# RWKV-6 attention ahead of a token/channel mixer: the read-out by 128-token chunks in place of 256-token units

## The chip, the cores and the metric

The kernel runs on one core of one Trainium2 chip. The metric is the device time of one execution in microseconds (us). A time given for a part comes from one profiled execution, counted from the start of its span. The engines are named PE (TensorE matmul), PEld (TensorE weight load), DVE (VectorE), ACT (ScalarE), POOL (GpSimd) and SP (SyncE, which issues most transfers).

## The reference

The inputs r, k, v, w have shape (4 batches, 8 heads, 768 tokens, 48). Each head carries a 48×48 state through the tokens; the result, laid out as (4, 768, 384), goes through a mixer over tokens and one over channels.

```python
for t in range(S):
    cur = einsum('bhd,bhe->bhde', u[None] * k[t], v[t])
    y[t] = einsum('bhd,bhde->bhe', r[t], state + cur)
    state = w[t][..., None] * state + einsum('bhd,bhe->bhde', k[t], v[t])
# x = y as (batch, tokens, heads * 48)
h = maximum(x.T @ w_tok1, 0) @ w_tok2          # over tokens, 768 -> 256 -> 768
u = x + h.T
out = u + maximum(u @ w_ch1, 0) @ w_ch2        # over channels, 384 -> 1536 -> 384
```

The mixer's weights arrive as 64-bit floats and are converted to 32 bits on the chip.

## The kernel before

**The attention** is done in 12 units of 256 tokens, three for each batch (`NU`, `UB`). A unit has two chunks of 128 tokens (`UC`), a chunk has two blocks of 64 tokens (`T`). Heads are handled in four pairs (`A`): one head of a pair lies in partitions 0 to 47, the other in 64 to 111 (`P` is 64). In the code q is the head of the pair and j the block of the chunk.

`levels(i)` forms the weights of every token upon every other inside a block of 64. It doubles the block length step by step: `gram` multiplies k and r on TensorE (line 246, and line 232 for the first step), `join` multiplies decays into k, r and w on VectorE (lines 271 to 273), and `pick` moves the wanted part of the product into the tile `at` (VectorE lines 238 and 255, ScalarE line 263).

`post(i)` then makes the unit's output, in these pieces:

- `tokens` transposes k on TensorE (line 306) and copies it out with ScalarE (line 307) as `kT`.
- `carry` multiplies kT and v (line 316) into the PSUM tile `kv`: for each block of 64 tokens, what it adds to the state. `update` forms the states, one for every block, on VectorE (lines 330 and 333).
- `before` multiplies r with the states (line 353) into the PSUM tile `y`. ScalarE then reads one column of it into the small tile `seen` (line 359), which `within` waits for.
- `within` adds the weights inside a block times v (line 366) to `y`; ScalarE copies the sum to `x` (lines 370 and 372).

`kv` and `y` take turns in the pool `ps_a`, which has one buffer of two PSUM banks. All these matmuls use 64 rows and 64 columns of the 128×128 array at a time. [...] For `within` the function `put` decides the latter: block j of head q goes to output half `j ^ q`, and the copies of line 372 bring the halves of the second head back into place.

**The mixer** (`mixing(bt)`) of a batch is: `hidden` (h1, line 386), `back` (line 393, added to x on VectorE in line 395), `turn` (transposes, lines 400 and 401), `up` (z, lines 408 and 410) and `down` (h2, lines 417 and 421). These matmuls use the whole array.

**The weights** are converted by `convert`, two blocks of 128×512 at a time, in six steps on VectorE and ScalarE (lines 168 to 174), with four buffers for the raw words.

**The order.** Pieces carry a weight, and `woven` merges lists of pieces in proportion to these weights. For batch 0 the levels of units 0 and 1 come first; then the levels of unit 2 with `post` of units 0 and 1, and `post` of unit 2, each woven with conversion steps; the hidden matmuls of batch 0 are set in between as their x chunks come. The rest of batch 0's mixer follows, then with batch bt's mixer the attention of batch bt + 1 is woven in. The scheduler of the language may still move single instructions between pieces where their operands allow it, within each engine's queue[...]. Units are loaded three ahead (`load_rkw`, `load_v`, both on SP's queue, issued at the end of `post`).

## Time and profile before

| what | value |
|---|---|
| time, median of 3 runs | 661.45 us (660.84 to 664.48) |
| time of the profiled execution | 661.45 us |
| its span | 659.7 us |
| PE busy | 622.7 us (94%) |
| DVE busy | 273.5 us (41%) |
| ACT busy | 194.9 us (30%) |
| line 366, `within` on PE | 768 records of 384 matmuls |
| line 333, state on DVE | 160 operations, 29.1 us busy |

The span is the time from the first to the last instruction of the program that the profile shows; 1.75 us of the execution lie around it. A busy time is the union of an engine's instructions[...]. An f32 matmul leaves two records on PE and two on PEld. The "chain" follows the work back from the last instruction to what released it; its pieces add up to the span. The clock granted to TensorE is given as a share of full speed.

### The profile page before, as it was taken

To read this page: it belongs to the slowest core of one execution; us is meant where nothing else is said; L and a number is where in the kernel's file an instruction comes from. 1 tells how busy PE (TensorE), PEld (TensorE's weight loads), DVE (VectorE), ACT (ScalarE), POOL (GpSimd) and SP (SyncE) were. 2 spreads that over 40 slices of the span, in tenths; PEclk is the share of its full clock that TensorE was granted. 3 is DMA by queue.
4 is the path that set the end of the run, shared out by engine and by line. 5 is a ranking of instruction groups with operands and counts; after the bars stand their busy time and mean duration, and the time that the engine had idled before them with its cause. 6 is when DMAs were issued, how large, how long until landed. Compare 5 with 4: busy or idle time off the path is not lost.

```text
span 659.7 us, 18806 instructions
## 1 busy us (share of the span) xinstructions
PE 622.7 (94%) x8584; PEld 456.6 (69%) x8584; DVE 273.5 (41%) x618; ACT 194.9 (30%) x465; POOL 7.2 (1%) x32
## 2 busy tenths in 40 slices
PE   3889789999999899999999999999999999999997
PEld 3777557867866666787686666788687565886854
DVE  6889789935555326242252226243143111000000
ACT  7153554512350431423231313432121201230200
POOL 3000000000000000000000000000000000000000
PEclk9996779999999899999999999999999999999999
DMA  8236755501030320101202220000000000000000
GB/s 348 79 99 193 203 141 171 191 0 51 27 107 18 109 62 2 50 2 50 73 2 61 63 74 1 2 2 2 14 14 14 13 26 0 1 1 12 13 24 24
DMA packets 19375, 38.56 MB, mean 58 GB/s; under 512 B 2112, under 2 KB 12864, under 8 KB 19296
## 3 DMA queue, kind: packets, MB, share of 16 engines
q1 hardware_dynamic: 19152, 37.36, 18.0%
q8 instruction: 67, 1.10, 0.7%
q14 instruction: 12, 0.10, 0.0%
q10 hardware_dynamic: 144, 0.00, 0.0%
HBM read 32.64 MB, written 4.72 MB: 57 GB/s over the span
## 4 chain that ended last, share of the span: by engine, by line
PE 88%; DVE 5%; ACT 3%; DMA 2%; issue 1%; SPq 0%; DVEq 0%; ACTq 0%
PE z_ps L408 29%; PE h_ps L417 29%; PE gram L246 10%; PE h_ps L386 6%; PE h_ps L393 5%; PE y_ps L353 2%; PE y_ps L366 2%; PE gram L232 2%; PE kv_ps L316 2%; PE kT_ps L306 1%; ACT at L263 1%; DMA d<-in_w_ch_dram 1%; DVE r L272 1%; PE xT_ps L400 1%; DMA w<-in_rkw_dram 1%
## 5 line engine op out<-in xcount | busy, mean ns | idle before, releaser
L408 PE MATMUL z_ps<-xT,wch 128*128 128x256 f32 x864 | 197.2, 384 | 0.6 <-ACT xT L401 0.6
L417 PE MATMUL h_ps<-wch,z 128*128 128x384 f32 x576 | 192.9, 491 | 0.8 <-ACT kT L307 0.8
L408 PEld LDWEIGHTS z_ps<-xT,wch 128*128 128x128 f32 x864 | 160.8, 190 | 23.7 <-ACT xT L401 0.8
L417 PEld LDWEIGHTS h_ps<-wch,z 128*128 128x128 f32 x576 | 107.8, 190 | 72.0 <-ACT kT L307 1.2
L410 ACT ACTIVATE z<-z_ps 128x256 f32<-128x256 f32 x144 | 55.1, 383 | 172.2 <-PE z_ps L408 172.2
L421 DVE TENSOR_TENSOR o<-x,h_ps 128x384 f32<-128x384 f32 x24 | 13.3, 554 | 200.6 <-PE h_ps L417 200.6
L246 PEld LDWEIGHTS gram<-r,k 48*64 48x64 f32 x3840 | 74.7, 155 | 23.3 <-issue 16.1
L246 PE MATMUL gram<-r,k 48*64 48x32 f32 x3840 | 81.8, 237 | 7.7 <-issue 3.1
L271 DVE TENSOR_TENSOR k<-k,decay 112x512 f32<-112x512 f32 x36 | 24.9, 691 | 58.8 <-PE gram L246 58.8
L386 PE MATMUL h_ps<-x,wtok 128*128 128x384 f32 x96 | 40.4, 571 | 1.7 <-ACT x L372 1.6
L263 ACT COPY at<-gram 16x256 f32<-16x256 f32 (+1 forms) x72 | 31.3, 434 | 32.9 <-PE gram L246 31.5
L393 PE MATMUL h_ps<-h,wtok 128*128 128x384 f32 x96 | 36.5, 508 | 3.4 <-DVE x L395 1.7
L271 DVE TENSOR_TENSOR k<-k,w 112x512 f32<-112x512 f32 x36 | 24.7, 687 | 35.5 <-PE gram L246 30.2
L333 DVE SCALAR_TENSOR_TENSOR state<-state,w_chunk,kv_ps 128x48 f32<-128x48 f32 x160 | 29.1, 258 | 11.0 <-PE kv_ps L316 10.9
L255 DVE COPY_PREDICATED at<-mask,gram 128x512 f32<-128x512 uint8 x36 | 32.3, 897 | 0.0
L238 DVE COPY_PREDICATED at<-mask,gram 128x512 f32<-128x512 uint8 x24 | 16.3, 723 | 37.2 <-PE gram L232 37.1
L232 PE MATMUL gram<-rp,kp 48*64 48x64 f32 x768 | 21.3, 250 | 10.5 <-ACT kp L220 8.0
L232 PEld LDWEIGHTS gram<-rp,kp 48*64 48x64 f32 x768 | 17.5, 155 | 17.8 <-ACT kp L220 10.4
L386 PEld LDWEIGHTS h_ps<-x,wtok 128*128 128x128 f32 x96 | 19.9, 219 | 13.9 <-issue 3.3
L272 DVE TENSOR_TENSOR r<-r,w 112x512 f32<-112x512 f32 x36 | 24.5, 685 | 6.7 <-ACT rp L216 6.7
L393 PEld LDWEIGHTS h_ps<-h,wtok 128*128 128x128 f32 x96 | 16.6, 189 | 14.8 <-DVE x L395 2.9
L359 ACT COPY seen<-y_ps 128x2 f32<-128x2 f32 x12 | 1.9, 160 | 79.4 <-PE y_ps L353 79.4
(55 smaller groups left out, 388.0 us busy)
## 6 DMA issues: line engine op xcount, KB each, us to landing
d<-in_w_ch_dram SPq DMA_DIRECT2D x10, 512.0 KB, 4.6
vt<-in_v_dram SPq DMA_DIRECT2D x12, 384.0 KB, 3.7
out_dram<-o SPq DMA_DIRECT2D x24, 192.0 KB, 1.9
x<-in_w_ch_dram SPq DMA_DIRECT2D x8, 512.0 KB, 4.2
w<-in_rkw_dram SPq DMA_DIRECT2D x18, 192.0 KB, 3.4
k<-in_rkw_dram SPq DMA_DIRECT2D x18, 192.0 KB, 3.2
r<-in_rkw_dram SPq DMA_DIRECT2D x18, 192.0 KB, 3.4
d<-in_w_tok_dram SPq DMA_DIRECT2D x4, 512.0 KB, 9.5
```

Source lines behind the costliest of these rows:

```text
L232: pe.matmul(g[cols, q, ts(a, T)], L["kp"][rows, tokens], L["rp"][rows, tokens], start=True, stop=True)
L246: fours(lambda q, j, rows, cols: pe.matmul(g[cols, q, ts(ca, 32)], k_[rows, ds(ca * 128 + j * T, T)], right[rows, ts(2 * ca + j, 32 // b), ...
L255: dve.copy_predicated(out=dst, data=g.rearrange("p q (m b) -> p q m b", b=b), mask=masks[l].rearrange("p x t -> p (x t)").rearrange("p (m ...
L263: act.copy(at[p:p + b, :, :, n * 2 * b + b:(n + 1) * 2 * b], g[p:p + b, :, :, ts(n, b)])
L271: dve.tensor_mul(left, left, wv[:, :, 1].unsqueeze(2).to_broadcast([ROWS, n, b]))
L272: dve.tensor_mul(right, right, wv[:, :, 0].unsqueeze(2).to_broadcast([ROWS, n, b]))
L333: dve.scalar_tensor_tensor(new[:, a], state[bt, g][:, a], L["w"][:, c, a, j:j + 1], got[:, a], op0=ALU.mult, op1=ALU.add)
L386: pe.matmul(sums[i], wtok1[:, c, ts(i, 128)], xs[bt][:, c, :], start=(c == 0), stop=(c == C - 1))
L393: pe.matmul(ps, wtok2[:, i, ts(c, 128)], h1[:, i, :], start=(i == 0), stop=(i == DTOK // 128 - 1))
L408: pe.matmul(ps, wch1[:, m, ts(jt, 128)], xT[:, m, ts(s, SEG)], start=(m == 0), stop=(m == DM // 128 - 1))
L410: act.activation(zs[s][:, jt, :], ps, AF.Relu)
L417: pe.matmul(ps, zs[s][:, jt, ts(n, 128)], wch2[:, jt, :], start=(jt == 0), stop=(jt == NJ - 1))
```

## The change

`post` works chunk by chunk. The functions `tokens`, `carry`, `before` and `within` take the chunk c and do half of what they did; `update` is gone, its work is at the end of `carry`. In `before` and `within`, block j of both heads goes to output half j, and `put` is gone, so a single copy brings y of a chunk to x. The state takes a multiply with a broadcast decay and an add, each over all four head pairs, in place of four operations that did both for one pair. `seen` is copied by halves. There are six state buffers before and five after; `kT` holds one chunk and has two buffers. In batch 0 the last two pieces of unit 2 (`before` and `within` of its second chunk) are taken out of the woven list and stand ahead of the fifth pair of hidden pieces, and the loads of unit 5 come after that pair.

The change is listed under the words "Weight conversion with three two-input VectorE operations, exponent in 16 bits through ScalarE, two pieces side by side, four raw-word buffers". The diff does not touch `convert`, which is so in both kernels.

```diff
-        def tokens():
+        def tokens(c):
...
-            L["kT"] = apool.tile([128, UC, A, 128], f32, name="kT", bufs=1)
...
+            L["kT"] = apool.tile([128, A, 128], f32, name="kT")
+            act.copy(L["kT"], ps)
...
+        def carry(c):
             L, vt = live[i], vs[i]
-            kv = L["kv"] = ps_a.tile([128, 2, 512], f32, name="kv_ps", tag="a")
...
+            kv = ps_a.tile([128, 2, 512], f32, name="kv_ps", tag="a")
+            for a in range(A):
+                for j, q in ((0, 0), (1, 1), (0, 1), (1, 0)):
+                    if not (last and j == 1):
+                        pe.matmul(kv[ts(q, P), j, ts(a, D)], L["kT"][ts(j, T), a, ts(q, P)],
+                                  vt[ts(j, T), c, ts(2 * a + q, D)], start=True, stop=True)
+            for j in range(1 if last else 2):
+                g = 2 * ch + j
+                new = apool.tile([128, A, D], f32, name="state", bufs=5)
+                got = kv[:, j, :A * D].rearrange("p (a e) -> p a e", a=A)
+                if g == 0:
+                    dve.tensor_copy(new, got)
+                else:
+                    dve.tensor_mul(new, state[bt, g], L["w"][:, c, :, j].unsqueeze(2).to_broadcast([128, A, D]))
+                    dve.tensor_add(new, new, got)
+                state[bt, g + 1] = new
-        def update():
...
-                        for a in range(A):
-                            dve.scalar_tensor_tensor(new[:, a], state[bt, g][:, a], L["w"][:, c, a, j:j + 1], got[:, a],
-                                                     op0=ALU.mult, op1=ALU.add)
...
-        pairs = ((0, 0), (1, 0), (1, 1), (0, 1))
-
-        def put(q, j):
-            return ts(j ^ q, T)
+        pairs = ((0, 0), (1, 1), (1, 0), (0, 1))
...
+        def before(c):
...
+            for a in range(A):
+                for q, j in got:
+                    pe.matmul(y[ts(j, T), q, ts(a, D)], r_[q * P:q * P + D, ds((c * A + a) * 128 + j * T, T)],
+                              state[bt, 2 * ch + j][q * P:q * P + D, a, :], start=(a == 0), stop=False,
+                              skip_group_check=True)
             seen = apool.tile([128, 2], f32, name="seen")
-            act.copy(seen, y[:, :, UC * A * D - 1])
+            for j in range(2):
+                if (0, j) in got:
+                    act.copy(seen[ts(j, T)], y[ts(j, T), :, A * D - 1])
...
-                for q, j in ((0, 0), (0, 1), (1, 1), (1, 0)):
-                    pe.matmul(y[put(q, j), q, ts(ca, D)], at[ts(j, T), q, ca, :], vt[ts(j, T), c, ts(2 * a + q, D)],
-                              start=False, stop=ca == 0, skip_group_check=True)
...
-            act.copy(x[:, 0], got[:, 0])
-            for n in range(2):
-                act.copy(x[ts(n, P), 1], got[ts(1 - n, P), 1])
+            for a in reversed(range(A)):
+                for q, j in pairs:
+                    pe.matmul(y[ts(j, T), q, ts(a, D)], at[ts(j, T), q, c * A + a, :],
+                              vt[ts(j, T), c, ts(2 * a + q, D)], start=(2 * ch + j == 0 and a == A - 1), stop=a == 0,
+                              skip_group_check=True)
+            act.copy(xs[bt][:, ch, :].rearrange("p (a q e) -> p q a e", a=A, q=2),
+                     y[:, :, :A * D].rearrange("p q (a e) -> p q a e", a=A))
...
-        return [(1.0, tokens), (1.1, carry), (0.1, update), (1.1, before), (1.1, within),
-                (0.01, lambda: load_rkw(i + 3)), (0.01, lambda: load_v(i + 3))]
+        pieces = []
+        for c in range(UC):
+            pieces += [(0.5, lambda c=c: tokens(c)), (0.5, lambda c=c: carry(c))]
+        for c in range(UC):
+            pieces += [(0.5, lambda c=c: before(c)), (1.0, lambda c=c: within(c))]
+        return pieces + [(0.01, lambda: load_rkw(i + 3)), (0.01, lambda: load_v(i + 3))]
...
-    p1[3:3] = hiddens[0] + hiddens[1]
-    p2[3:3] = hiddens[2] + hiddens[3]
+    p1[4:4] = hiddens[0] + hiddens[1]
+    p2[4:4] = hiddens[2] + hiddens[3]
     emit(woven(levels(2), p0 + p1, to_tok[:2]))
-    emit(woven(p2, to_tok[2:]))
-    emit(hiddens[4] + hiddens[5])
+    emit(woven(p2[:-4], to_tok[2:]))
+    emit(p2[-4:-2] + hiddens[4] + p2[-2:] + hiddens[5])
```

## The prediction

> **What bounds the kernel now.** I read the page first, for the engine shares. TensorE is the engine that sets the time:

> ```profile
> PE 622.7 (94%) x8584; PEld 456.6 (69%) x8584; DVE 273.5 (41%) x618; ACT 194.9 (30%) x465; POOL 7.2 (1%) x32
> ...
> PE 88%; DVE 5%; ACT 3%; DMA 2%; issue 1%; SPq 0%; DVEq 0%; ACTq 0%
> ```

> TensorE is busy 94% of the 659.7 us, and 88% of the chain that ended last is TensorE work. The second view is the table of windows, by stage (columns: stretch, length, then busy us of PE, PEld, DVE, ACT, POOL; the clock granted to TensorE; DMA share; GB/s):

> ```profile
> 39.00:53.00 14.00, 12.31 (x365) 11.14 (x362) 12.84 (x33) 6.26 (x14) 0.11 (x1) 0.79 0.37 90
> 53.00:75.00 22.00, 18.86 (x419) 13.34 (x416) 18.28 (x49) 10.65 (x24) 0.11 (x1) 0.67 0.69 216
> 75.00:92.00 17.00, 14.25 (x320) 10.69 (x319) 13.75 (x36) 7.49 (x16) 0.11 (x1) 0.70 0.55 157
> ...
> 265.00:391.00 126.00, 125.11 (x1780) 92.77 (x1781) 39.18 (x96) 35.16 (x88) 0.22 (x2) 1.00 0.16 44
> ```

> There are two regimes. From 39 to 92 us batch 0's attention runs with little mixer work beside it: TensorE and VectorE are both loaded (45.4 and 44.9 us of 53), the clock is low, and one waits for the other. Later, as in 265 to 391 us, TensorE is idle for 0.9 us of 126: every nanosecond added to its stream is paid in full. VectorE and ScalarE have two thirds of that stretch free.

> The third view is the chain of waits in order of time (start, length, what); it prices TensorE's work in place:

> ```profile
> 49.50 1.96 PE y_ps L366 x64
> ...
> 105.75 31.45 PE z_ps L408 x144
> ...
> 304.27 1.06 PE y_ps L353 x48
> ...
> 315.83 1.08 PE y_ps L366 x64
> 316.90 0.92 PE gram L246 x64
> ...
> 338.80 1.08 PE kv_ps L316 x64
> 339.87 4.08 PE z_ps L408 x18
> ...
> 356.81 1.08 PE y_ps L353 x64
> ...
> 379.19 1.06 PE kv_ps L316 x47
> ```

> Each f32 matmul leaves two records. Three readings. (a) The attention matmuls use a quarter of the array each (64 rows by 64 columns); 64 such records after another attention group add 0.92 us (316.90). (b) The groups with 48 records take 1.06 us, as long as those with 64 (1.06 to 1.08). Line 353 at 304.27 belongs to a first unit, where chunk 0 has no state for its first 64 tokens; line 316 at 379.19 is a last unit (the row merges 47 of its 48). By the code, 16 of the 48 records in each use only two of the four quarters and 32 use all four, so the fullest quarter holds 8 + 8 = 16 records, as in the group of 64. The time of a group is therefore the records on its **fullest quarter**, 0.92 / 16 = 0.058 us each, not its number of records. (c) A lone attention group between mixer matmuls costs more than its 0.92: z alone runs at 31.45 / 144 = 0.218 us a record, so 18 should take 3.93; the pair at 338.80 took 1.08 + 4.08, that is 1.23 for the group, 0.31 above 0.92. That is the price of a **switch** from full array to quarters and back.

> [...] 64 records of line 366 took 1.96 us at 49.50 and 1.08 at 315.83.

> **The change, part by part.** The words given name the weight conversion; the diff leaves `convert` alone, and VectorE's instructions of lines 168 to 174 are the same in number. So that part costs nothing, in any cover. What changes is `post`: it works by chunks of 128 tokens where it worked by units of 256.

> 1. *Quarters in `within`.* Before, `put` sends the output to half j^q, so rows j and columns j^q visit all four quarters. After, rows j and columns j: only the two on the diagonal. Each chunk's 16 matmuls are 32 records on two quarters, 16 on each: by (b) 0.92 us a chunk instead of 0.46. `before` (rows q, columns j) and `carry` (rows j, columns q) still visit four. Price: 0.92 us a unit at full clock. Nine units run in the full regime: 9 × 0.92 = **8.3 us**. In batch 0, units 0 and 2 ran at half clock and unit 1 (1.19 in the chain) at full: 1.84 + 0.92 + 1.84 = **4.6 us**.

> 2. *More groups.* `tokens`, `carry`, `before` and `within` come twice as often, half as long. Counting in the two instruction orders, attention groups between full-array work after the first z rise from 80 to 93 (many new halves fall beside a gram group and cost no switch): 13 × 0.31 = **4.0 us**.

> 3. *Waits for the one kv/y buffer.* It is filled 48 times instead of 24. In a unit: carry 1 waits for VectorE to have read kv of chunk 0; `before` 0 for kv of chunk 1; `before` 1 for ScalarE's copy of y of chunk 0. [...] In the full regime the order puts three z matmuls (6 records, 1.3 us) between carry 1 and `before` 0 of a batch's first unit, against two adds and a multiply (3 × 0.36 = 1.1, and what else stands in VectorE's queue); in other units a gram group or 2 to 12 h matmuls. At the end of a batch one h1 matmul (two records of 0.32, from 7.94 us for 24 h records in the chain) covers the copy of 0.48. I take 0.5 us in each of three batches, **1.5 us**; bounds 0 and 5. In batch 0 cover is thin: per unit one more wait for `seen` (49.26 to 49.50, 0.24) and one for the copy (0.48 + 0.05), some 0.7 × 3 = **2 us**; bounds 0 and 6.

> 4. *ScalarE.* Three copies of y a unit (0.48 + 2 × 0.47 = 1.43) become two of 128×384 (0.48 each), and `seen` becomes up to four of 0.16: 1.6 us before, 1.6 after; no change in load. But the last chunk's x is ready one copy after its matmul rather than three: the wait of h1 for line 372 (one of 1.6 us, at 68.17) mostly goes, **−1 us**.

> 5. *VectorE.* 160 scalar_tensor_tensor, busy 29.1 us, so 0.73 for a state of four, become 40 multiplies and 40 adds on 128×192. No row has these; 112×256 took 0.42, 112×128 0.31, a PSUM copy of 128×192 0.356. I take 0.36, bounds 0.31 and 0.42: 0.72 a state, −0.1 to +0.1. It hides under TensorE later; over 12 states of batch 0 it is ±1.3 us, taken as 0. Carry of chunk 0 can start before chunk 1 is transposed, but in batch 0 VectorE's new order puts conversion steps between the state steps, so the last state of unit 0 ends at about the old time; credit 0, bounds −3 and +1.3.

> 6. *Moved work.* SP issues the same transfers; conversion loads now stand ahead of some k loads, and the loads of unit 5 come after the fifth hidden. The table of waits has VectorE waiting for conversion data twice, 2.1 us in all, so the loads are mostly early: 0, bounds −2 and +3. POOL's one step in a unit, the memset of `w_chunk`, waits for the last state operation as before, with nothing queued behind that is late. `kT` and the state buffers (5 for 6) hold as many live tiles as a chunk needs: 0.

> Sum: 8.3 + 4.6 + 4.0 + 1.5 + 2 − 1 = 19.4. The profiled execution took 661.45 us (span 659.7), which is the median of the three runs: 661.45 + 19.4 = **680.9, say 681**.

> **Rivals.**
> - *Batch 0 absorbs its share.* 39 to 105.75 us holds about 10.2 us of idle TensorE (1.7 + 3.1 + 2.8 + 2.6). If the slower `within` fills it, only 8.3 + 4.0 remain: 673.7. Against it: line 366 stands in the chain there.
> - *The single buffer becomes the bound.* 24 more turns with VectorE's or ScalarE's queue in front, at 0.7 us each uncovered, is 17 in place of my 3.5: 694. Against it: the order has full-array work between most halves.
> - *Faster.* The chunked carry frees batch 0: if all 10.2 us of idle go and a pair of diagonal quarters costs nothing extra, 661.45 − 10.2 + 4.0 = 655. It decides only where `within` on two quarters costs under 10.2 − 4.0 − 3.3 = 2.9 us in all, against my 12.9; reading (b) speaks against.
> - *Nothing of it matters:* 661. It would need two-quarter groups free and the switches hidden; TensorE idles 0.9 us in 126.

> **How the numbers follow.** What a measurement can tell from no change is 0.5%, 3.3 us. My sum 0.71, its own range 674 to 688; absorbed 0.14; buffer-bound 0.10; faster 0.03; no change 0.02. A range of 671 to 692 leaves out most of the buffer case's upper half and the last two. Slower by over 0.5%: 0.95.

> **What would show it.** The line that replaces 366 should show 32 records in about 0.92 us net (1.06 to 1.08 alone) in the full regime; TensorE busy up by some 14 to 17 us; ups and downs of the mixer unchanged per record; a few waits of PE for `state` adds and for the x copy, under 1 us each; the first z some 5 to 6 us later than 105.75. I am wrong in step 1 if two-quarter groups of 32 take near 0.5 us, in step 3 if the waits on the buffer sum to over 5 us, and in the batch 0 part if the first z starts within 2 us of its old place.

## The result, and the profile after

| | before | after |
|---|---|---|
| median | 661.32 us of 4 runs (660.84 to 664.48) | 678.39 us of 4 runs (677.19 to 678.80) |
| profiled execution, its span | 661.45, 659.7 us | 678.03, 676.3 us |

The changed kernel takes 1.0245 times as long (95% interval 1.021 to 1.028): slower by 17 us where 19.4 were forecast, 678.4 for 681. The changed page, its first part and the engines' shares of the chain that ended last:

```profile
PE 639.9 (95%) x8584; PEld 468.8 (69%) x8584; DVE 270.8 (40%) x538; ACT 193.9 (29%) x485; POOL 7.2 (1%) x32
...
PE 86%; DVE 9%; issue 3%; ACT 1%; DMA 1%; SPq 0%; DVEq 0%; ACTq 0%
```

TensorE has the same 8584 records and is busy 17.2 us longer. VectorE and ScalarE are busy 2.7 and 1.0 us less, and the kernel is slower all the same. The group of `within`, line 366 before and now line 352:

```profile
L366 PE MATMUL y_ps<-vt,at 64*64 64x48 f32 x768 | 15.4, 234 | 1.8 <-ACT seen L359 1.8
...
L352 PE MATMUL y_ps<-vt,at 64*64 64x48 f32 x768 | 32.1, 240 | 6.1 <-issue 3.4
```

Records and shape are as before. The busy time, a union in which matmuls side by side count once, was 15.4 us and is 32.1. The 768 records come to 179.7 us one by one before (768 × 234 ns) and to 184.3 after, so about half as many run side by side. The idle time ahead of the group has grown too, from 1.8 to 6.1 us, 3.4 us of it with no releaser ("issue"). In the chain of waits of the changed kernel, each kind of attention group (the last two rows follow on each other, the first three stand alone between mixer matmuls):

```profile
306.50 1.06 PE y_ps L352 x32
...
338.85 0.61 PE kv_ps L317 x32
...
350.24 0.61 PE y_ps L339 x32
...
358.79 1.01 PE y_ps L352 x30
...
359.85 0.92 PE gram L246 x62
```

Three kinds of group have 32 records. A quarter is here one half of the operands' partitions together with one half of the output's; in the table of lines the records of `carry` and `within` have 64*64 of the array, those of `before` 48*64, those of the mixer 128*128. `carry` (317) and `before` (339), on four quarters, take 0.61 us. `within` (352), on two, takes 1.06, as long as the 64 of before (1.08). The windows by stage, in the same stretches as before except the last, which is the second batch's stage (columns: stretch, length, busy us of PE, PEld, DVE, ACT, POOL, clock, DMA share, GB/s):

```profile
39.00:53.00 14.00, 12.42 (x281) 10.37 (x279) 12.67 (x28) 5.24 (x13) 0.11 (x1) 1.00 0.37 107
53.00:75.00 22.00, 18.44 (x492) 15.95 (x491) 15.92 (x37) 9.33 (x22) 0.11 (x1) 0.77 0.56 169
75.00:92.00 17.00, 12.91 (x283) 10.20 (x284) 9.81 (x21) 6.13 (x17) 0.11 (x1) 0.70 0.45 134
92.00:105.75 13.75, 13.35 (x66) 7.59 (x67) 6.89 (x15) 6.93 (x16) 0.00 (x0) 0.74 0.29 80
273.00:428.00 155.00, 153.99 (x2149) 110.64 (x2148) 53.01 (x102) 44.53 (x115) 0.22 (x2) 1.00 0.14 40
```

The clock of the first row has to be read with care. The trace's record of the clock begins at 58.2 us here, and the view takes what lies ahead of it as full. TensorE was slow there too, by its chain:

```profile
48.25 1.97 PE y_ps L352 x32
```

A group of 32 such records took 1.06 us at 306.50, so it took 1.86 times as long here. The second batch's stage in the kernel before, by its own window:

```profile
265.20:416.80 151.60, 149.77 (x2146) 108.41 (x2146) 53.28 (x122) 44.52 (x111) 0.22 (x2) 1.00 0.15 41
```

In that stage TensorE is busy 4.22 us longer on the same work. Three units of quarters at 0.92 and 5 more groups at 0.31 make 2.76 + 1.55 = 4.31. Its idle time fell from 1.8 to 1.0 us, so the stage grew by 3.4. Cut at the first z matmul of each batch, to 0.1 us, the profiled executions compare so (us; the groups are those between full-array work, counted in the instruction order, which the two kinds of split below change):

| kernel | to the first z | stage 1 | stage 2 | stage 3 | rest | groups by stage |
|---|---|---|---|---|---|---|
| before | 105.6 | 159.6 | 151.6 | 146.1 | 96.8 | 29, 30, 21 |
| after | 112.5 | 160.5 | 155.0 | 151.5 | 96.8 | 31, 35, 27 |
| difference | +6.9 | +0.9 | +3.4 | +5.4 | 0 | +2, +5, +6 |

So 6.9 of the 16.6 us between the two profiled executions arise before the first z, and 9.7 after it.

### The profile page after: what moved, and what is told of

The parts are those of the page before. It is cut to its first block, busy times and chain, and to the rows that moved or that the text cites. A ratio compares the mean times of both kernels' runs of the same rounds, so it can differ in the third digit from the quotient of the medians.

```text
span 676.3 us, 18764 instructions
## 1 busy us (share of the span) xinstructions
PE 639.9 (95%) x8584; PEld 468.8 (69%) x8584; DVE 270.8 (40%) x538; ACT 193.9 (29%) x485; POOL 7.2 (1%) x32
## 4 chain that ended last, share of the span: by engine, by line
PE 86%; DVE 9%; issue 3%; ACT 1%; DMA 1%; SPq 0%; DVEq 0%; ACTq 0%
PE h_ps L405 28%; PE z_ps L396 25%; PE gram L246 10%; PE h_ps L374 5%; PE h_ps L381 5%; PE y_ps L352 4%; PE y_ps L339 2%; PE kv_ps L317 2%; PE gram L232 2%; DVE k L271 1%; PE kT_ps L305 1%; DVE r L272 1%; PE xT_ps L388 1%; DVE wch L174 1%; DVE at L255 1%
## 5 line engine op out<-in xcount | busy, mean ns | idle before, releaser
L396 PE MATMUL z_ps<-xT,wch 128*128 128x256 f32 x864 | 200.7, 385 | 0.4
L396 PEld LDWEIGHTS z_ps<-xT,wch 128*128 128x128 f32 x864 | 159.6, 190 | 24.7 <-ACT z L398 3.0
L246 PEld LDWEIGHTS gram<-r,k 48*64 48x64 f32 x3840 | 75.5, 154 | 22.2 <-issue 15.1
L246 PE MATMUL gram<-r,k 48*64 48x32 f32 x3840 | 83.1, 236 | 5.2 <-DVE at L255 1.7
L352 PEld LDWEIGHTS y_ps<-vt,at 64*64 64x64 f32 x768 | 29.0, 155 | 15.3 <-issue 8.9
L352 PE MATMUL y_ps<-vt,at 64*64 64x48 f32 x768 | 32.1, 240 | 6.1 <-issue 3.4
L232 PE MATMUL gram<-rp,kp 48*64 48x64 f32 x768 | 19.8, 247 | 10.3 <-ACT kp L220 8.0
L238 DVE COPY_PREDICATED at<-mask,gram 128x512 f32<-128x512 uint8 x24 | 16.4, 721 | 26.6 <-PE gram L232 26.6
L345 ACT COPY seen<-y_ps 64x2 f32<-64x2 f32 x44 | 6.8, 154 | 66.3 <-PE y_ps L339 66.1
```

Source lines behind the costliest of these rows:

```text
L232: pe.matmul(g[cols, q, ts(a, T)], L["kp"][rows, tokens], L["rp"][rows, tokens], start=True, stop=True)
L246: fours(lambda q, j, rows, cols: pe.matmul(g[cols, q, ts(ca, 32)], k_[rows, ds(ca * 128 + j * T, T)], right[rows, ts(2 * ca + j, 32 // b), ...
L352: pe.matmul(y[ts(j, T), q, ts(a, D)], at[ts(j, T), q, c * A + a, :], vt[ts(j, T), c, ts(2 * a + q, D)], start=(2 * ch + j == 0 and a == A ...
L396: pe.matmul(ps, wch1[:, m, ts(jt, 128)], xT[:, m, ts(s, SEG)], start=(m == 0), stop=(m == DM // 128 - 1))
```

## The experiments

Theory: `within` pays for its fullest quarter, and each added group for its switch. Rivals: the single kv/y buffer, the state in two operations, and, for the start, something other than the quarters. Ratios are to the kernel before, measured on the same chip. The runs were made on several chips, among which the median of the kernel before lies between 661.32 and 663.59 us, so the small differences are read from the traces.

### Four quarters again in the changed kernel

```diff
+        def put(q, j):
+            return ts(j ^ q, T)
...
-                    pe.matmul(y[ts(j, T), q, ts(a, D)], r_[
+                    pe.matmul(y[put(q, j), q, ts(a, D)], r_[
...
-                for q, j in pairs:
-                    pe.matmul(y[ts(j, T), q, ts(a, D)], at[
+                for q, j in ((0, 0), (0, 1), (1, 1), (1, 0)):
+                    pe.matmul(y[put(q, j), q, ts(a, D)], at[
...
-            act.copy(xs[bt][:, ch, :]...)
+            act.copy(x[:, 0], sum_[:, 0])
+            for n in range(2):
+                act.copy(x[ts(n, P), 1], sum_[ts(1 - n, P), 1])
```

> The changed kernel with one thing put back: block j of head q again goes to output half j^q, so that within visits all four quarters of the array (and three copies of y a chunk put the halves in order, as before). Quarter theory: the fullest quarter of a chunk's within holds 8 records instead of 16, so 0.46 us less a chunk at full clock: 24 x 0.46 = 11 us less than the changed kernel, 13 with the half clock of batch 0, less about 1 us for the two more copies that stand before the next chunk; 665 to 668 us. Rival, the single kv/y buffer: the same number of turns of the buffer and longer copies, so 678 us or a little more. Rival, switches alone: three more attention groups than the changed kernel, 678 to 680 us.

Measured: 670.08 us, ratio 1.0111 (1.0074 to 1.0147). The chain of this kernel:

```profile
304.28 0.61 PE y_ps L358 x32
...
311.53 0.61 PE y_ps L342 x32
```

`within` (358) is back at 0.61. The stages are 2.3, 2.8 and 2.7 us shorter than in the changed kernel, 7.8 in all with two more groups, where nine units at 0.92 make 8.3. The first z, however, stays at 112.6. `seen` follows the new places. The quarters cost what they should in the full regime and nothing visible in batch 0: there something else holds the start back.

### Two quarters in the kernel before

```diff
-        pairs = ((0, 0), (1, 0), (1, 1), (0, 1))
+        pairs = ((0, 0), (1, 1), (1, 0), (0, 1))
...
-            return ts(j ^ q, T)
+            return ts(j, T)
...
-                for q, j in ((0, 0), (0, 1), (1, 1), (1, 0)):
+                for q, j in pairs:
...
-            act.copy(x[:, 0], got[:, 0])
-            for n in range(2):
-                act.copy(x[ts(n, P), 1], got[ts(1 - n, P), 1])
+            for q in range(2):
+                act.copy(x[:, q], got[:, q])
```

> The kernel before with one part of the change alone: output half j in place of j^q in before and within, so within visits the two diagonal quarters; the copies of y to x need no shift. Units stay at 256 tokens, kv and y take as many turns, the state is computed as before. Quarter theory: 32 records on each of two quarters in a unit in place of 16 on four: 0.92 us a unit, nine units 8.3 us, and 2.8 to 4.6 us in batch 0 according to its clock: 672 to 675 us. Rival (the buffer, the groups and the waits carry the loss): within 2 us of 661 us.

Measured: 670.58 us, ratio 1.0136 (1.0098 to 1.0175). The chain:

```profile
306.35 1.06 PE y_ps L353 x47
...
317.91 1.94 PE y_ps L366 x62
```

The unit's records of line 366 (62 of its 64 stand in this row) take 1.94 us where they took 1.08, and line 353, which still visits four quarters, keeps its 1.06. In stage 2 TensorE is busy 152.59 us for 149.77, 2.82 more, where 2.76 were said. The stages grow by 0.2, 2.6 and 2.6; the first z comes 1.8 us later, not 4.6. (The first stage has no half-clock stretch here. Before had one of 3.4 us at 224.7, worth about half of that, an estimate from the 64 records of line 366 that took 1.96 us in a half-clock stretch and 1.08 at full clock.)

### Two quarters in `before` instead of `within`

```diff
-            got = [(q, j) for q, j in pairs if 2 * ch + j > 0]
+            got = [(q, j) for q, j in ((0, 0), (1, 1), (0, 1), (1, 0)) if 2 * ch + j > 0]
...
-                    pe.matmul(y[ts(j, T), q, ts(a, D)], r_[
+                    pe.matmul(y[ts(q, T), j, ts(a, D)], r_[
...
-                    pe.matmul(y[ts(j, T), q, ts(a, D)], at[
+                    pe.matmul(y[ts(q, T), j, ts(a, D)], at[
```

The copies to x and `seen` follow the new places.

> The changed kernel with the output half chosen by head (half q) instead of by block: now within (rows j, columns q) visits all four quarters and before (rows q, columns q) only the two diagonal ones. Four copies a chunk bring y into place. It has the same 96 attention groups after the first z as the run that put back j^q (670.1 us). If a matmul group is priced by its fullest quarter, whoever it is, five of six chunks of before pay 0.46 us each: 20 x 0.46 = 9 us, or 7 if batch 0 absorbs its share: 677 to 680 us. If the loss belongs to within alone (its operands, or the wait for y), it goes here: 669 to 672 us.

Measured: 678.21 us, ratio 1.0222 (1.0144 to 1.0301), as slow as the change. The chain:

```profile
306.44 0.61 PE y_ps L352 x32
...
313.69 1.06 PE y_ps L339 x32
```

The two durations have changed places. Which output half goes with which operand half decides, 1.06 us against 0.61, not what is computed.

### One kv and one y buffer for a unit

```diff
-            kv = ps_a.tile([128, 2, 512], f32, name="kv_ps", tag="a")
+            if c == 0:
+                L["kv"] = ps_a.tile([128, 2, 512], f32, name="kv_ps", tag="a")
+            kv = L["kv"][:, :, ds(c * A * D, A * D)]
```

and the same for y: the two chunks use different columns of one buffer, so it is filled 24 times again.

> The changed kernel, but kv and y of both chunks of a unit lie side by side in one tile (chunk 1 in columns 192 to 383), so the buffer turns 24 times and not 48; all else, groups and quarters too, as in the changed kernel. Quarter theory and my sum: the extra waits for the buffer are small: 0 to 3 us less than the changed kernel, most of it in batch 0: 675 to 678 us. Buffer rival: most of the 17 us goes: 662 to 666 us.

Measured: 678.15 us, ratio 1.0246 (1.0214 to 1.0277). The stages are those of the changed kernel within 0.1 us, the first z comes at 112.3. The buffer rival falls for the later stages. For batch 0 this run cannot tell, since TensorE's stop at its end, treated below, is in it as well (3.25 us) and hides other waits. Without this run the waits of TensorE in the changed kernel's second stage (waiting instruction, releaser, us in total, times, longest) already speak against it:

```profile
PE kT_ps L305 <- DVE k L271: 0.9, 2, 0.5
```

That is the whole table: no wait for kv or y.

### The state in its old form

```diff
-                    dve.tensor_mul(new, state[bt, g], L["w"][:, c, :, j].unsqueeze(2).to_broadcast([128, A, D]))
-                    dve.tensor_add(new, new, got)
+                    for a in range(A):
+                        dve.scalar_tensor_tensor(new[:, a], state[bt, g][:, a], L["w"][:, c, a, j:j + 1], got[:, a],
+                                                 op0=ALU.mult, op1=ALU.add)
```

> The changed kernel with the states computed as in the kernel before (four scalar_tensor_tensor a state in place of a multiply and an add). My theory: VectorE is off the path, so 678 us, within 2 us. Rival (VectorE's longer chain in batch 0 sets the late start of the mixer): 2 to 5 us less.

Measured: 676.14 us (674.04 to 681.04), ratio 1.02 (1.0128 to 1.0271): not told apart from the change. The first z came at 111.2, later stages within 0.4 us.

### More groups without the quarters

The kernel before, with `carry`, `before` and `within` in four pieces each, woven in among the mixer's work with larger weights; each matmul is the same and goes to the same place.

```diff
-        return [(1.0, tokens), (1.1, carry), (0.1, update), (1.1, before), (1.1, within),
+        def quarters(w, f):
+            return [(w / 4, lambda n=n: f(n)) for n in range(4)]
+
+        return [(1.0, tokens), *quarters(3.0, carry), (0.1, update), *quarters(3.0, before), *quarters(3.0, within),
```

> The kernel before with carry, before and within handed to the weaver in four pieces each (same matmuls, same quarters, same tiles and same turns of the buffer) with larger weights, so that mixer matmuls come between the pieces. In the instruction order the attention groups between full-array work after the first z are 112 in place of 80. If a switch costs 0.31 us a group: 32 x 0.31 = 10 us more, 671 us (668 to 674). If the array changes its mode for nothing and the 0.31 of the trace belongs to something else: within 2 us of 661.

Measured: 671.78 us, ratio 1.0147 (1.0117 to 1.0178). Groups after the first z are 37, 42 and 33, 32 more than before; the stages grow by 2.4, 3.5 and 3.8 us, 9.7 in all, 0.30 for each. Of stage 3's 3.8, some 1.7, half its length by the same estimate, belong to a half-clock stretch of 3.4 us at 524.1, which the kernel before does not have there; without it 8.0 are left, 0.25 for each. The cleanest is stage 2, which has no half-clock stretch in either kernel:

```profile
269.00:424.10 155.10, 153.49 (x2149) 108.42 (x2147) 53.55 (x123) 44.34 (x110) 0.22 (x2) 1.00 0.13 37
```

TensorE busy 153.49 against 149.77 us for 12 more groups is 0.31 each. The switch is priced by a run now, at 0.25 to 0.31 us, and lies in TensorE's own time.

### What holds the start: two loads held back

The chain of the changed kernel at the end of batch 0's attention:

```profile
83.04 0.67 ACT kp L216
...
84.89 0.55 PE y_ps L352 x12
85.44 3.42 issue
88.87 0.99 PE y_ps L352 x14
```

In the middle of one group of `within`, after 12 of its records, TensorE does nothing for 3.42 us, with no semaphore it waits for. The next records use the same operands. The timeline has SP issue k, w and two conversion loads d (512 KB each) one behind the other between 78.4 and 81.0. The DMA view of that stretch, 80 to 85.4 us, and then of 85.4 to 89:

```profile
## 3 DMA queue, kind: packets, MB, share of 16 engines
q1 hardware_dynamic: 457, 1.56, 97.6%
```

```profile
q1 hardware_dynamic: 34, 0.09, 6.1%
q8 instruction: 1, 0.02, 1.7%
```

In this stretch, while data fills the 16 DMA engines, no packet of the instruction queue passes; one comes when they run free, from 86.5 to 87.4 us by the trace, the one before it having come at 73.9. (It is no fixed rule: in the kernel before one came at 80.4, after the same two d loads had been issued and before they had landed.) Over the whole span q8 has 67 packets, 1.10 MB, so 16.4 KB each, and the 17,168 records of PE and PEld are 256 for each packet.

The traces let one count where TensorE stops. Take all its instructions that the trace holds, in order of start. The stop at 85.44 comes after 3521 of them. In the fourteen kernels of this document TensorE stands still 44 times for over 0.4 us with no semaphore to wait for. Every time its count differs from 3521 by a multiple of 256, and every time it goes on 1.2 to 1.6 us after the next packet in turn has landed (here 1.46, from 87.41 to 88.87). Read together, the counts and the landings say that TensorE waits for its next block of 256 instructions, here for 3.42 us.

Whether the data loads keep the packet back is the next question. Both d loads are made to wait until y of the first chunk of unit 2 has been copied to x (ScalarE first writes a word into each row of their buffers, and the loads overwrite it):

```diff
             d64 = bits64[(first + n) % 4]
+            if hold is not None:
+                act.copy(d64.bitcast(f32)[:, 0:1], hold)
...
-            emit(woven(turned, to_ch[:2]))
+            held = [(0.2, lambda: convert(first_ch, 0, xs[0][:, 4, 0:1]))]
+            emit(woven(turned, held + to_ch[1:2]))
```

> The changed kernel, but the two 512 KB loads of the first channel weights, which start at 80.2 us there, are held until the copy of y of chunk 0 of unit 2 is done (a one-column copy into their buffer before them). It asks about the 3.4 us in which TensorE stands still at 85.4 us in the middle of a within, waiting for nothing that the trace shows. Theory A: its next 16 KB of instructions come late behind these loads; then the stop shrinks to under 1 us and the end of batch 0's attention comes 2 to 3 us sooner; the weights are converted later, so the total may keep 675 to 679 us. Theory B: the stop belongs to the order of instructions (a wait that the profile doesn't show): it stays at 3 us.

Measured: 671.80 us, ratio 1.0122 (1.0052 to 1.0193). The windows of this kernel:

```profile
75.00:92.00 17.00, 15.65 (x350) 11.87 (x347) 10.09 (x20) 8.23 (x23) 0.11 (x1) 0.89 0.50 129
92.00:105.75 13.75, 12.74 (x108) 7.22 (x108) 12.65 (x25) 7.14 (x15) 0.00 (x0) 1.00 0.50 155
```

TensorE is busy 15.65 us of 17 where the change had 12.91, the 3.4 us stop is gone, and the clock is full from 92 us on where it was 0.74. The first z comes at 107.8, 4.7 us earlier, and stage 1 is 1.9 shorter. A stop of 0.5 us is left at the same place. The wait also shifts some of the order on TensorE and ScalarE, so this run alone doesn't separate the stop from that.

### An eighth of the same loads

This kernel keeps TensorE's instructions and leaves out seven eighths of the data of the two loads, so that old words are converted in their place.

```diff
-            sp.dma_start(d64.rearrange("p (c k) -> p c k", c=dst.shape[1]), src)
+            words = 2 * PIECE // dst.shape[1] // part
+            sp.dma_start(d64.rearrange("p (c k) -> p c k", c=dst.shape[1])[:, :, :words], src[:, :, :words])
...
-            emit(woven(turned, to_ch[:2]))
+            eighth = [(0.2, lambda: convert(first_ch, 0, 8))]
+            emit(woven(turned, eighth + to_ch[1:2]))
```

> The changed kernel with an eighth of the two loads of the first channel weights: 64 KB each in place of 512 KB, at the same place of the queue (the rest of these two weight blocks is left out, so stale words are converted in its place). TensorE's instructions and their order are those of the changed kernel. Theory A (TensorE's next instructions come late behind these loads): the loads end some 3 us sooner, so the stop of 3.4 us at 85.4 us goes to under 1 us, the half clock that follows it goes too, and the first z matmul comes 3 to 5 us before 112.5. If the gain lasts, 671 to 675 us. Theory B (an order or a wait that the profile doesn't show): the stop stays at about 3 us and the time at 678.

Measured: 675.23 us, ratio 1.0167 (1.0091 to 1.0243). The chain at the same place:

```profile
87.01 0.55 PE y_ps L353 x12
87.56 0.24 issue
87.80 0.64 PE y_ps L353 x14
```

The same matmuls, less data ahead of them: 3.42 becomes 0.24 us, and the instruction packet now comes at 85.2, lands at 86.5, and TensorE goes on 1.3 us later. That the loads make the stop is shown, and with the count above, that a late instruction packet stands between: TensorE goes on 1.46 us after it there and 1.3 here. The first z came only 1.4 us earlier, at 111.1. But this execution was already behind before its shortened loads were issued, at 81.8 us. The transposes of k of unit 2, in the changed kernel and here:

```profile
76.57 1.71 PE gram L305 x8
```

```profile
78.22 1.71 PE gram L306 x8
```

From there to the first z it is 35.9 us in the changed kernel and 32.9 here, 3.0 less, which is about what the stop lost (3.2). Half clock is here as well, from 88.2 to 98.5 us.

### Both undone, and the hold alone

Four quarters and the held loads together, and the held loads in the kernel before; the edits are those above.

> The changed kernel with both suspects gone: output half j^q again, and the first channel weights held until y of chunk 0 of unit 2 is copied. If the two are independent, their gains add: -8.3 for the quarters (670.1 against 678.4) and -6.6 for the hold (671.8 against 678.4): 663 to 665 us, level with the kernel before, the rest being 15 more attention groups at 0.31. If the hold gained only because within was slow, 667 to 670 us.

> A control: the kernel before with the same hold of the first channel weights. It has no stop at 85 us to remove, so if the gain of the hold is the stop of the changed kernel, this is 661 to 665 us, or somewhat slower since weights arrive later. If holding the loads is good in itself (less traffic beside the attention of batch 0), 655 to 659 us, which would beat both.

Measured: 664.19 us, ratio 1.0008 (0.9985 to 1.0031), and 662.91 us, ratio 0.9999 (0.9978 to 1.0021). Together they bring the chunked kernel level with the one before, while the hold gives the kernel before nothing: its longest stop without a semaphore is 0.95 us, and 0.64 beside these loads. By the price of a switch it should not be quite level, for it still has 15 more groups than before, 3.8 to 4.7 us at 0.25 to 0.31. Its profiled stages are 4.5 us longer, but the medians leave room for 2.1 at most. What gives the rest back is not shown. From the held loads to both, the first z goes from 107.8 to 106.3, so with the stop away the quarters of batch 0 are worth 1.5 us.

### Fewer groups than before

If a switch costs 0.31 us, merging neighbouring attention pieces of the kernel before ahead of the weaving, four by four or two by two, might gain:

```diff
+            all_ = att
+            att = [(sum(c for c, _ in all_[k:k + 4]), lambda k=k: emit(all_[k:k + 4])) for k in range(0, len(all_), 4)]
             emit(woven(att, pieces))
```

> The kernel before with four successive attention pieces handed to the weaver as one where it weaves them with the mixer (batches 1 to 3), so that attention groups stand together: 59 groups between full-array work after the first z in place of 80. Switch theory at 0.31 us a group: 6.5 us less than before, 655 us, less what longer runs of dependent pieces wait for each other (0 to 5 us): 655 to 660 us. If waits win: 661 to 668 us.

> The kernel before with two successive attention pieces handed to the weaver as one in batches 1 to 3; mostly one step of levels and one piece of post, which don't wait for each other. 69 groups between full-array work after the first z in place of 80. Switch theory: 11 x 0.31 = 3.4 us less, 659 to 661 us against some 663, which would beat both kernels. Rival, from the run with four pieces (674 us with 59 groups): pieces that stand together wait for VectorE and cost more than the switches give, 664 to 668 us.

Measured: 674.04 us, ratio 1.0159 (1.0099 to 1.0219), by fours, and 663.86 us, ratio 1.0021 (0.9998 to 1.0045), by twos. Groups fell to 59 and 69, as meant, and neither gains. Stage 2 by fours:

```profile
271.60:426.80 155.20, 148.62 (x2149) 109.61 (x2147) 52.87 (x123) 44.48 (x110) 0.22 (x2) 1.00 0.14 40
```

TensorE is busy 1.15 us less than before for 8 fewer groups, 0.14 each, under half of what an added group cost. And it is idle 6.6 us for 1.8. In the waits of that stage the largest are these:

```profile
PE gram L246 <- DVE r L272: 2.6, 4, 0.9
PE h_ps L417 <- issue: 1.5, 1, 1.5
PE kv_ps L316 <- issue: 1.1, 1, 1.1
```

The first was 0.6 in the same stage before: attention steps that stand together no longer have mixer matmuls between them to cover VectorE. The other two make as much together. They are stops for an instruction block by the count above, here at a DMA share of 0.14 over the stage; what makes the blocks late there was not shown. No version that was run beats the kernel before.

## Why the prediction was right, point by point

**What bounds.** Right. TensorE gained 17.2 us busy, some 14 to 17 were said, and no gain from the relief of VectorE and ScalarE (2.7 and 1.0 us) can be seen.

**Step 1, quarters.** Right in the full regime: 32 records of `within` take 1.06 us alone, as said, 0.45 more than 32 on four quarters. Nine units: 8.3 forecast, 7.8 measured by putting the four quarters back. The pricing by the fullest quarter held when the loss was moved to `before` (0.61 became 1.06 us there). Mis-sized in batch 0: 4.6 forecast, 1.8 in the kernel before with two quarters, 1.5 in the chunked kernel with the loads held, and none with the stop there. The assumption that failed is that batch 0's group is paid in full because it stands in the chain.

**Step 2, switches.** Right for added groups: 80 became 93, and the price of 0.31 read from one pair of lines came out as 0.31 in the clean stage and 0.25 over all 32. Taken away, a group gave back less, 0.14. In the changed kernel itself, the 9.7 us after the first z less 7.8 for the quarters leave 1.9 where 4.0 were forecast; the half-clock stretch that the kernel before had in stage 1, worth 1.7 by estimate, makes up most of the gap.

**Step 3, the buffer.** 3.5 us forecast. Of the 1.5 after the first z nothing was measured: giving each unit one buffer again left those stages within 0.1 us, and no wait for kv or y stands in the second stage's table. That the mixer matmuls between the halves cover it fits the order in that step; 0 was the lower bound given. Of the 2 in batch 0 the one-buffer run says little, since the stop is in it. With stop and quarters both undone the first z comes 0.7 us later than before, and that is what is left there for this step and all smaller ones together.

**Steps 4 and 5.** Small, as said. ScalarE's wait at h1 for the last copy is out of the table of waits; the old form of the state was not told apart from the new.

**Step 6, moved work.** The term that failed: it was taken as 0 with bounds of −2 and +3, because the loads were said to be mostly early in the old kernel. They were not early at this place. The chain of the kernel before has:

```profile
77.46 6.65 DMA d<-in_w_ch_dram
```

In the changed order k, w and the two d loads go out together, and TensorE stops for 3.42 us in the middle of a group. Half clock sets in as the stop begins, at 85.5 us. Holding the loads back gave 4.7 us before the first z and 6.6 in the profiled executions. The question asked was only whether VectorE would wait for the data; whom the data delays on the way was not asked. The edit of the order at the end of batch 0 is not the cause: it moves no instruction past another on any engine.

**The sum.** To the first z, 4.6 + 2 − 1 = 5.6 was forecast and 6.9 came, close by luck: quarters and waits put too high met a stop put at nothing. After it, 8.3 + 4.0 + 1.5 = 13.8 was forecast and 9.7 came. Of the 4.1, 1.5 are the buffer. The other 12.3 are 3.4, 4.3 and 4.6 by stages, from three units of quarters and 2, 5 and 6 groups, against 0.9, 3.4 and 5.4 measured. Stage 1: before had 3.4 us of half clock at 224.7, worth 1.7 by estimate, which did not come again, and TensorE idled 1.1 less. Stage 2: it idled 0.8 less. Stage 3 took 0.8 more, 0.4 of it idle time.

**The rivals.** "Batch 0 absorbs its share" was right of the quarters there and wrong of the time, since another loss took the place. The single buffer as a bound, no change, and faster all fell.

**The clock.** The two durations of the same 64 records in the prediction, 1.96 and 1.08 us, show two speeds and not what brings them about; the last two rows of this document speak against idleness as the only cause.

**Open.** How the 6.6 us of the hold divide. Counted from the transposes of k, where both executions were 1.65 us behind the changed kernel, the first z came 3.0 us sooner with an eighth of the loads and 6.4 with the hold. So about 3 are the stop. The other 3.4 are shared in an unknown way by half clock (none after 78.9 us with the hold) and the order that the hold shifts, and the 1.9 of stage 1 have no cause shown. These are single executions, and the intervals of the two runs overlap. Also open is why the half-clock stretches fall where they do.

## What to carry to other kernels

Price packed matmuls by the records on the fullest quarter of the array (here 16 records took 0.92 us after another attention group), and each added return to full-array work as a switch (0.25 to 0.31 us here); then check in the stage's own windows that TensorE has no idle time to hide them (1.0 of 155 us here). When an edit moves loads, ask not only whether their readers will wait, but what else needs the DMA engines in those microseconds (here an instruction packet, at 3.42 us). Taking switches away gained nothing in the two runs that tried it; by fours, the merged groups waited for VectorE (2.6 us at line 272, for 0.6) and for instructions (1.5 and 1.1 us). When TensorE stands still with nothing to wait for, count its instructions and look at when the instruction queue's packets land (here 1.2 to 1.6 us before it went on).

## What the runs showed of the hardware that was not expected

```profile
79.00:85.40 6.40, 5.74 (x191) 4.46 (x191) 5.48 (x13) 3.88 (x12) 0.11 (x1) 1.00 0.94 273
85.40:88.90 3.50, 0.08 (x4) 0.03 (x2) 1.70 (x4) 0.00 (x0) 0.00 (x0) 0.52 0.08 29
```

Half clock began 0.1 us into the stop, after 6.4 us of which TensorE was busy for 5.74. After 88.87 us TensorE was busy nearly without a break (13.35 of 13.75 us from 92 us on) and stayed at half clock for 10.3 us, three times 3.4.
